# Top-32 attention and two MoE layers on one core: the masking Prelu takes the 32nd score with scale -1, and v's scale is taken off when the transposed x leaves PSUM

## The chip, the cores and the metric

One core of a Trainium2 chip. The metric is the device time of one execution in microseconds (us). Engines: PE = TensorE (matrix multiply), PEld = its weight loads, DVE = VectorE, ACT = ScalarE, POOL = GpSimd, SP = SyncE, which issues the DMAs.

## The reference, cut to what matters

Attention with the 32 largest scores of each row, four batches, eight heads, 576 positions of 64 numbers, then two MoE-like layers on 2304 tokens of 512 numbers:

```
scores = q @ k.T / sqrt(64)
kth    = the 32nd largest score of each row
scores = where(scores >= kth, scores, -1e9)
attn   = exp(scores - max);  attn = attn / (sum(attn) + 1e-9)
x      = attn @ v                              # heads side by side: 2304 x 512
h      = max(x @ w_in, 0);   x = (h * h) @ w_out            # 512 -> 2048 -> 512
out    = max(x @ w1, x @ w2, x @ w3) @ w_out2               # 512 -> 768 -> 512
```

The arithmetic is carried in pairs: a rounded number and what the rounding lost (`xh` and `xl`, `hh` and `hl`, two halves of `wt`, of `qt`, of `e16`, of `vt`), so that three matmuls stand for one.

## The kernel before, in words

**Jobs.** `attend` is called for a unit (some query tiles of one batch) and a pair of heads. A job in it is one tile of 128 queries for one head, or, at the 64 queries that are left over, 64 of each of two heads. There are 144 jobs, 24 for each of six groups. A job runs so:

- TensorE makes 576 scores for each of 128 queries in two halves (L499); ScalarE copies them to `s`, scaled (L426).
- VectorE finds the 32 largest in four rounds: MAX8 writes eight into `mx` (L432), MATCH_REPLACE8 strikes them out in the copy `w` (L434). The 32nd is `mx[:, 31:32]`.
- POOL makes two columns of `nb`: the negated 32nd score (L436), and the 32nd score minus the largest plus a constant (L438).
- ScalarE: Prelu with the bias `nb[:, 0:1]` and the slope 2^110 (L440, recorded as L308): scores at or above the 32nd keep their distance to it, the others become hugely negative. Then Exp with the bias `nb[:, 1:2]` (L442), then a cast to 16 bits (L445).
- POOL makes the lost part of that cast (L446 to L449, recorded as L305, the line of a helper).
- SyncE issues a transposing DMA, `e16` to `et` (L450); TensorE multiplies `et` with `vt` (L461), ScalarE copies the result to `xs` (L464). The first column of `vt` is ones, so `xs` also holds the sums.

**Scale of v.** `prep_v`, once for each of 16 pairs of heads, measures the size of v: ScalarE sums its absolute values (L371), TensorE sums over the partitions (L374), ScalarE copies that to `sc` (L375), and VectorE turns it by bit operations into a power of two that scales v up (L376). ScalarE multiplies v by it (L378) before v is cut into two 16-bit halves. `sc` lives on until the last use of the pair: `finish_x` multiplies the sums by it (L504, on VectorE, with `sc` as a pointer operand, one number for each partition) and takes the reciprocal (L506), and POOL multiplies `xs` by that (L512), so that x is back at its own size in `xg`.

**x.** TensorE transposes `xg` into PSUM (L484; L470 for the left-over queries), ScalarE copies it to `xh` (L486, L473), and VectorE subtracts that copy from PSUM into `xl` (L487 and L474, recorded as L305 with `xt<-b`).

**MoE.** `moe(g)` runs when the x of a group is complete: 654 matmuls (L595) over 28 pieces of weights. For the first group the weights come as 64-bit numbers and are converted on the way, 56 half pieces: ScalarE (L553, recorded as L308 with `cv`), VectorE (L555 and L557), ScalarE (L559), POOL (`wt<-cv,wt`), and the result is also written to DRAM; the other five groups read that.

**What sets the order.** Every operation is handed to `Plan` with its engine, a modelled duration, a priority and the buffers that it reads and writes. `Plan.run` places the operations one after the other where they can start earliest in this model (a hop of some 200 to 280 ns between engines, a small weight for the priority), and the program is then emitted in that order, which `fix_order` keeps on each engine. A buffer kind has a number of slots (`nbufs`: `mx` 4, `nb` 4, `e` 3, `e16` 2, `et` 2, `sc` 6); an operation that opens a buffer waits for the last use of the one that had the slot. So each engine's queue is a fixed list, and the list depends on all modelled durations and on all reads and writes.

Of the kernel before, what the change touches and what calls it, by code (L numbers as in the profile page):

```python
# [10 lines left out]
F32 = mybir.dt.float32  # L11
# [20 lines left out]
LW, LI = 20.0, 0.001  # L32
DROP = 2.0 ** 110
SL = 1000.0
# [228 lines left out]
def kernel(ctx, tc, q, k, v, w_in, w_out, w1, w2, w3, w_out2, out):  # L263
# [8 lines left out]

    nbufs = {"ks": 1, "qs": 1, "vst": 2, "kt": 4, "qt": 1, "vt": 4, "vs": 1, "sm": 2, "sc": 6, "s": 6, "w": 2, "e": 3, "e16": 2,
             "et": 2, "mx": 4, "nb": 4, "rc": 4, "xs": 2, "xr": 2, "xg": 3, "xt": 3, "cv": 3,
# [94 lines left out]
    def prep_v(vst):  # L369
# [4 lines left out]
        pe(A_V, 107.0, [sm], [ps, sc], lambda: nc.tensor.matmul(ps[:, 0:1], ones_t[:], sm[:], start=True, stop=True))  # L374
        act(A_V, 1, [ps], [sc], lambda: nc.scalar.activation(sc[:], ps[:, 0:1], AF.Copy, bias=2.0 ** -100))  # L375
        dve(A_S, 1, [sc], [sc], lambda: nc.vector.tensor_scalar(  # L376
            sc[:].bitcast(U32), sc[:].bitcast(U32), 0x7F800000, 0x7F800000, op0=ALU.bitwise_and, op1=ALU.bitwise_xor))
# [6 lines left out]
            nc.gpsimd, vt[:, :, :, VW2:VW], vs[:], vt[:, :, :, 1:VW2]))  # L384
        return vt, sc

# [14 lines left out]
    def attend(i, unit, p):  # L401
# [7 lines left out]
        if new:  # L409
            kv[b, p] = [kt, *prep_v(load_v(b, p))]  # L410
        kt, vt, sc = kv[b, p]
        if g not in xt:
# [7 lines left out]
        for j, h in jobs:  # L420
            s = buf("s", [P, S])
            for f in range(2):
# [4 lines left out]
                    s[:, cs], ps[:, 0:HS], AF.Copy, scale=escale))  # L427
            w_, mx, nb, e = buf("w", [P, S]), buf("mx", [P, 32]), buf("nb", [P, 2]), buf("e", [P, S])
            for r in range(4):
# [3 lines left out]
                if r < 3:  # L433
                    dve(A_X, S, [src, (mx, r)], [w_], lambda src=src, mx=mx, m8=m8, w_=w_: nc.vector.match_replace(  # L434
                        out=w_[:], in_to_replace=mx[:, m8], in_values=src[:], imm_value=-3.0e38))
            gps(A_E, 1, [(mx, 3)], [(nb, 0)], lambda mx=mx, nb=nb: nc.gpsimd.tensor_scalar(  # L436
                nb[:, 0:1], mx[:, 31:32], -1.0, None, op0=ALU.mult))
            gps(A_E, 1, [(mx, 0), (mx, 3)], [(nb, 1)], lambda mx=mx, nb=nb: nc.gpsimd.tensor_scalar(  # L438
                nb[:, 1:2], mx[:, 31:32], mx[:, 0:1], ebias, op0=ALU.subtract, op1=ALU.add))
            act(A_E, S, [s, (nb, 0)], [e], lambda s=s, e=e, nb=nb: prelu(  # L440
                e[:], s[:], DROP, bias=nb[:, 0:1]), psum=False, ptr=1)
            act(A_E, S, [e, (nb, 1)], [e], lambda nb=nb, e=e: nc.scalar.activation(  # L442
                e[:], e[:], AF.Exp, bias=nb[:, 1:2]), psum=False, ptr=1)
            e16, et = buf("e16", [P, 2 * S], F16), buf("et", [P, 10, P], F16)
# [21 lines left out]
            if j < 0:  # L466
                xr = buf("xr", [P, P])
                finish_x(xs, sc, D, 1, xr, lambda xr=xr: xr[0:D, :].unsqueeze(1))
                ps = buf("b", [P, 512])
                pe(A_X, 107.0, [xr], [ps, (xh, (p, "r")), (xl, (p, "r"))], lambda xr=xr, ps=ps: nc.tensor.transpose(  # L470
                    ps[:, 0:D], xr[0:D, :], ident_t[0:D, 0:D]))
                cs = slice(rcol[b], rcol[b] + D)
                act(A_X, D, [ps], [(xh, (p, "r"))], lambda ps=ps, cs=cs: nc.scalar.copy(xh[:, p, cs], ps[:, 0:D]))  # L473
                dve(A_S, D, [ps, (xh, (p, "r"))], [(xl, (p, "r"))], lambda ps=ps, cs=cs: sub(  # L474
                    nc.vector, xl[:, p, cs], ps[:, 0:D], xh[:, p, cs].bitcast(F32)), slack=SL / 2)
            elif h == 1 and (j % 2 == 1 or j == nt - 1):
                j0 = j - j % 2
                finish_x(xs, sc, P, j + 1 - j0, xg, lambda j0=j0, j=j: xg[:, j0:j + 1, :])
        w = nt * P
        ps = buf("b", [P, 512])  # L480

        def f():
            for c in range(nt):
                nc.tensor.transpose(ps[:, c * P:(c + 1) * P], xg[:, c, :], ident)  # L484
        pe(A_S, 107.0 * nt, [xg], [ps, (xh, (p, col)), (xl, (p, col))], f)
        act(A_S, w, [ps], [(xh, (p, col))], lambda: nc.scalar.copy(xh[:, p, col:col + w], ps[:, 0:w]))  # L486
        dve(A_S, w, [ps, (xh, (p, col))], [(xl, (p, col))], lambda: sub(  # L487
            nc.vector, xl[:, p, col:col + w], ps[:, 0:w], xh[:, p, col:col + w].bitcast(F32)), slack=SL / 2)

# [11 lines left out]

    def finish_x(xs, sc, pn, nt, dst, xo):
        rc = buf("rc", [P, 2, 2, 1])
        dve(A_S, 4, [xs, sc], [rc], lambda: nc.vector.tensor_scalar(  # L504
            rc[0:pn, 0:nt], xs[0:pn, 0:nt, :, 0:1], eguard, sc[0:pn, :], op0=ALU.add, op1=ALU.mult), slack=SL)
        dve(A_S, 4, [rc], [rc], lambda: nc.vector.reciprocal(rc[0:pn, 0:nt], rc[0:pn, 0:nt]))  # L506

        def part(x):
            return xs[0:pn, 0:nt, :, 1 + x * D:1 + (x + 1) * D]
        n = nt * 2 * D  # L510
        gps(A_X, n, [xs], [xs], lambda: nc.gpsimd.tensor_tensor(part(0), part(0), part(1), op=ALU.add))
        gps(A_X, n, [xs, rc], [dst], lambda: nc.gpsimd.tensor_tensor(  # L512
            xo().rearrange("p t (h d) -> p t h d", h=2), part(0),
            rc[0:pn, 0:nt].to_broadcast([pn, nt, 2, D]), op=ALU.mult))
# [237 lines left out]
```

## Time and profile before

| | |
|---|---|
| times of three runs | 1120.74, 1124.24, 1127.41 us; median 1124.24 |
| profiled execution | 1117.19 us, its span 1115.0 us |
| TensorE busy | 962.4 us (86%), weight loads 893.1 (80%) |
| VectorE busy | 887.4 us (80%) |
| ScalarE busy | 743.0 us (67%) |
| GpSimd busy | 676.8 us (61%) |
| mean granted TensorE clock | 0.914 |
| HBM | 200.80 MB read, 34.08 MB written |

The span goes from the first to the last instruction of the program; the execution's own time is a little longer. A share of the span is an average over stages that have different limits, so the shares alone don't name the limit: the page's second part, with 40 slices, shows VectorE full from the start to some 860 us and TensorE full from some 420 us to the end.

### The profile page before, as it was taken

The numbers are of one execution on the slowest core, as the hardware profiler recorded it, in microseconds if no ns is written. First come the engines' busy times: TensorE is split into PE (matmuls) and PEld (weight loads), VectorE is DVE, ScalarE is ACT, GpSimd is POOL, SyncE is SP. The second block draws the span as 40 slices with busy tenths as digits, with TensorE's granted clock in tenths as the row PEclk, the third lists the DMA queues.
The fourth block names the chain that finished last, engine by engine and source line by source line (L and its number), as shares of the span: only waits on it lengthen the run. The fifth ranks groups of instructions, "written<-read, shape, count | busy, mean of one in ns | idle before, by whom it ended". The sixth has DMA issues, their size and how long they took to land.

```text
span 1115.0 us, 18581 instructions
## 1 busy us (share of the span) xinstructions
PE 962.4 (86%) x6116; PEld 893.1 (80%) x6116; DVE 887.4 (80%) x1840; ACT 743.0 (67%) x1572; POOL 676.8 (61%) x979
## 2 busy tenths in 40 slices
PE   3455537977787799999999999999999999999998
PEld 2344426866677589999899999899999999989997
DVE  7999999999999999999999999999999800100020
ACT  7866757778886778887788877887856743123321
POOL 6854668979889768766576777676655531112211
PEclk8555557998888899999999999999999999999999
DMA  7633586789999899999999999989999987776663
GB/s 292 148 79 70 135 278 156 278 244 316 268 283 301 266 360 269 283 293 288 280 270 268 284 288 232 293 230 267 252 264 260 268 256 264 260 257 241 269 245 141
DMA packets 221343, 278.56 MB, mean 250 GB/s; under 512 B 175680, under 2 KB 179776, under 8 KB 199744
## 3 DMA queue, kind: packets, MB, share of 16 engines
q1 hardware_dynamic: 221248, 277.39, 84.5%
q8 instruction: 48, 0.79, 0.3%
q14 instruction: 47, 0.39, 0.1%
HBM read 200.80 MB, written 34.08 MB: 211 GB/s over the span
## 4 chain that ended last, share of the span: by engine, by line
PE 56%; DVE 27%; POOL 5%; issue 4%; ACT 4%; DMA 4%; SPq 0%; POOLq 0%; ACTq 0%; DVEq 0%
PE a L595 35%; PE b L595 13%; DVE mx L432 11%; DVE w L434 9%; PE b L499 4%; PE b L461 4%; DVE cv L557 3%; DMA et<-e 2%; DVE rc L504 1%; POOL wt L305 1%; DVE cv L555 1%; POOL hl L305 1%; POOL e L305 1%; DMA out_dram<-ot 1%; DVE m L646 0%
## 5 line engine op out<-in xcount | busy, mean ns | idle before, releaser
L432 DVE MAX8 mx<-w 128x8 f32<-128x576 f32 x432 | 310.6, 743 | 0.1
L305 POOL TENSOR_TENSOR e<-e,e 128x512 f16<-128x512 f32 (+1 forms) x288 | 213.6, 757 | 72.6 <-ACT e L445 52.4
L595 PE MATMUL a<-xt,wt 128*128 128x384 f32 x1296 | 249.4, 346 | 0.5 <-DVE xt L305 0.3
L595 PE MATMUL b<-xt,wt 128*128 128x384 f32 x1152 | 234.1, 345 | 2.9 <-DVE xt L305 1.2
L595 PEld LDWEIGHTS a<-xt,wt 128*128 128x128 f32 x1296 | 229.8, 193 | 1.4 <-POOL wt L305 0.7
L595 PE MATMUL a<-hh,wt 128*128 128x384 f32 x768 | 225.2, 344 | 0.5 <-ACT hh L621 0.4
L434 DVE MATCH_REPLACE8 w<-mx,w 128x576 f32<-128x576 f32 x288 | 211.9, 738 | 0.0
L595 PEld LDWEIGHTS b<-xt,wt 128*128 128x128 f32 x1152 | 203.8, 192 | 5.2 <-DVE xt L305 1.6
L305 POOL TENSOR_TENSOR hl<-r,hh 128x384 fp32r<-128x384 f32 x96 | 98.4, 1025 | 136.9 <-ACT hh L621 115.6
L499 PE MATMUL b<-kt,qt 128*128 128x288 f32 x640 | 138.3, 345 | 41.5 <-ACT xs L464 12.7
L499 PEld LDWEIGHTS b<-kt,qt 128*128 128x128 f32 x640 | 116.2, 224 | 52.1 <-ACT xs L464 16.5
L461 PEld LDWEIGHTS <-et 128*128 128x128 f16 (+1 forms) x1440 | 85.5, 109 | 79.1 <-DMA et<-e 49.4
L308 ACT ACTIVATE e<-s,nb 128x576 f32<-128x576 f32 x144 | 111.6, 777 | 54.8 <-POOL nb L436 43.6
L461 PE MATMUL b<-vt,et 128*128 128x129 f16 (+3 forms) x1440 | 102.2, 224 | 52.7 <-DMA et<-e 38.3
L595 PEld LDWEIGHTS a<-hh,wt 128*128 128x128 f32 x768 | 142.3, 189 | 1.8 <-ACT hh L621 1.4
L595 PE MATMUL a<-hl,wt 128*128 128x384 f32 x384 | 132.0, 344 | 8.8 <-POOL hl L305 8.6
L426 ACT ACTIVATE s<-b 128x288 f32<-128x288 f32 x288 | 107.2, 408 | 13.2 <-PE b L499 12.2
L442 ACT ACTIVATE e<-e,nb 128x576 f32<-128x576 f32 x144 | 112.1, 778 | 2.4
L434 DVE MATCH_REPLACE8 w<-mx,s 128x576 f32<-128x576 f32 x144 | 106.0, 738 | 0.0
L619 ACT ACTIVATE r<-b 128x384 f32<-128x384 f32 x96 | 47.0, 490 | 88.5 <-PE b L595 86.5
L432 DVE MAX8 mx<-s 128x8 f32<-128x576 f32 x144 | 105.0, 741 | 1.1 <-POOL nb L438 1.1
L445 ACT CAST e<-e 128x576 f16<-128x576 f32 x144 | 97.0, 676 | 9.3 <-DMA et<-e 9.0
(59 smaller groups left out, 1291.1 us busy)
## 6 DMA issues: line engine op xcount, KB each, us to landing
wt<-wsc SPq DMA_DIRECT2D x140, 1024.0 KB, 5.5
wsc<-wt SPq DMA_DIRECT2D x28, 1024.0 KB, 6.1
xt<-in_moe_w_out_dram SPq DMA_DIRECT2D x22, 512.0 KB, 4.9
ks<-in_k_dram SPq DMA_DIRECT2D x16, 576.0 KB, 4.9
xt<-in_moe_w_dram SPq DMA_DIRECT2D x18, 512.0 KB, 4.9
xt<-in_moe_w_in_dram SPq DMA_DIRECT2D x16, 512.0 KB, 5.1
qs<-in_q_dram SPq DMA_DIRECT2D x16, 384.0 KB, 4.1
vst<-in_v_dram SPq DMA_DIRECT2D x16, 320.0 KB, 4.7
```

The lines of the kernel that those rows point to most:

```text
L305: eng.tensor_tensor(out_ap, a, b, op=ALU.subtract)
L308: return nc.scalar.activation(out_ap, src, AF.Prelu, alpha=slope, **kw)
L426: act(A_S, HS, [ps], [(s, f)], lambda s=s, cs=cs, ps=ps: nc.scalar.activation(s[:, cs], ps[:, 0:HS], AF.Copy, scale=escale))
L432: dve(A_X, S, [src], [(mx, r)], lambda src=src, mx=mx, m8=m8: nc.vector.max(out=mx[:, m8], in_=src[:]))
L434: dve(A_X, S, [src, (mx, r)], [w_], lambda src=src, mx=mx, m8=m8, w_=w_: nc.vector.match_replace(out=w_[:], in_to_replace=mx[:, m8], in_va ...
L442: act(A_E, S, [e, (nb, 1)], [e], lambda nb=nb, e=e: nc.scalar.activation(e[:], e[:], AF.Exp, bias=nb[:, 1:2]), psum=False, ptr=1)
L445: act(A_E, S, [e], [(e16, 0)], lambda e=e, e16=e16: nc.scalar.copy(e16[:, S:2 * S], e[:]), psum=False)
L461: nc.tensor.matmul(ps[0:m, 0:wv], et[:, mm_, c0:c1], vt[:, hh, vc, 0:wv], start=x == 0, stop=x == 8)
L499: nc.tensor.matmul(ps[:, 0:HS], a, c, start=m == 0, stop=m == len(seq) - 1)
L557: dve(C_D, 512, [raw, cv], [cv], lambda part=part, cv=cv: nc.vector.scalar_tensor_tensor(cv[:], part(0), 29, cv[:], op0=ALU.logical_shift_ ...
L595: nc.tensor.matmul(o, x, y, start=first and i == 0 and m == 0, stop=last and i == n - 1 and m == 2)
L619: act(MA, N, [ps], [r], lambda r=r, ps=ps: nc.scalar.activation(r[:, 0:N], ps[:, 0:N], AF.Relu))
```

## The change: what it does

- The Prelu takes `mx[:, 31:32]` itself as its bias and multiplies the score by -1, so it works on the 32nd score minus the score. Its slope for negative values is now 2^-100 (`KEEP`), and the Exp multiplies by -2^100, which brings the kept scores back and makes the others hugely negative. POOL's negated column (L436) goes; `nb` has one column. The Prelu reads `mx`, which POOL alone read before.
- `prep_v` makes a second power of two, `us`, from the same sum, by one more operation on VectorE. `sc` is read no more after `prep_v`; it gets 2 slots in place of 6, and `us` gets 6.
- `finish_x` multiplies the sums by the constant 2 in place of `sc`. x thus stays scaled in `xg` and in PSUM.
- When it leaves PSUM, ScalarE's copy to `xh` becomes an activation with the scale `us` (a pointer), and VectorE's subtraction becomes a multiplication by `us` with a subtraction (scalar_tensor_tensor).

```diff
--- before.py
+++ after.py
@@ -30,7 +30,7 @@
 HOP = 180.0
 TICK = 10240.0 / 3.0
 LW, LI = 20.0, 0.001
-DROP = 2.0 ** 110
+KEEP = 2.0 ** -100
 SL = 1000.0
 DBW, DL0, DL1, DTR = 360.0, 1280.0, 900.0, 1500.0
 HP = 1.4
@@ -270,7 +270,7 @@
     ebias = ESHIFT * float(np.log(2.0))
     eguard = 1e-9 * 2.0 ** ESHIFT
 
-    nbufs = {"ks": 1, "qs": 1, "vst": 2, "kt": 4, "qt": 1, "vt": 4, "vs": 1, "sm": 2, "sc": 6, "s": 6, "w": 2, "e": 3, "e16": 2,
+    nbufs = {"ks": 1, "qs": 1, "vst": 2, "kt": 4, "qt": 1, "vt": 4, "vs": 1, "sm": 2, "sc": 2, "us": 6, "s": 6, "w": 2, "e": 3, "e16": 2,
              "et": 2, "mx": 4, "nb": 4, "rc": 4, "xs": 2, "xr": 2, "xg": 3, "xt": 3, "cv": 3,
              "hh": 6, "hl": 6, "r": 2, "m0": 1, "m1": 1, "ot": 2, "wt": 4,
              "b": 4, "a": 4}
@@ -373,6 +373,9 @@
         ps = buf("b", [P, 512])
         pe(A_V, 107.0, [sm], [ps, sc], lambda: nc.tensor.matmul(ps[:, 0:1], ones_t[:], sm[:], start=True, stop=True))
         act(A_V, 1, [ps], [sc], lambda: nc.scalar.activation(sc[:], ps[:, 0:1], AF.Copy, bias=2.0 ** -100))
+        us = buf("us", [P, 1])
+        dve(A_S, 1, [sc], [us], lambda: nc.vector.tensor_scalar(
+            us[:].bitcast(U32), sc[:].bitcast(U32), 0x7F800000, None, op0=ALU.bitwise_and))
         dve(A_S, 1, [sc], [sc], lambda: nc.vector.tensor_scalar(
             sc[:].bitcast(U32), sc[:].bitcast(U32), 0x7F800000, 0x7F800000, op0=ALU.bitwise_and, op1=ALU.bitwise_xor))
         act(A_V, 10 * D, [vst, sc], [vs], lambda: nc.scalar.activation(
@@ -382,7 +385,7 @@
         act(A_V, 10 * D, [vs], [(vt, 1)], lambda: nc.scalar.copy(vt[:, :, :, 1:VW2], vs[:]), psum=False)
         gps(A_V, 10 * D, [vs, (vt, 1)], [(vt, 2)], lambda: sub(
             nc.gpsimd, vt[:, :, :, VW2:VW], vs[:], vt[:, :, :, 1:VW2]))
-        return vt, sc
+        return vt, us
 
     def prep_q(i, unit, p):
         b, tl, rem = unit[:3]
@@ -408,7 +411,7 @@
         plan.bias = 0
         if new:
             kv[b, p] = [kt, *prep_v(load_v(b, p))]
-        kt, vt, sc = kv[b, p]
+        kt, vt, us = kv[b, p]
         if g not in xt:
             t = buf("xt", [P, 2, KD, NW], F32R)
             xt[g] = Half(t, 0), Half(t, 1)
@@ -425,7 +428,7 @@
                 pe(A_S, c_mm(HS) * (2 if j >= 0 else 4), [kt, qt], [ps, (s, f)], scores(j, h, nt, qt, kt, ps, cs))
                 act(A_S, HS, [ps], [(s, f)], lambda s=s, cs=cs, ps=ps: nc.scalar.activation(
                     s[:, cs], ps[:, 0:HS], AF.Copy, scale=escale))
-            w_, mx, nb, e = buf("w", [P, S]), buf("mx", [P, 32]), buf("nb", [P, 2]), buf("e", [P, S])
+            w_, mx, nb, e = buf("w", [P, S]), buf("mx", [P, 32]), buf("nb", [P, 1]), buf("e", [P, S])
             for r in range(4):
                 src = s if r == 0 else w_
                 m8 = slice(8 * r, 8 * r + 8)
@@ -433,14 +436,12 @@
                 if r < 3:
                     dve(A_X, S, [src, (mx, r)], [w_], lambda src=src, mx=mx, m8=m8, w_=w_: nc.vector.match_replace(
                         out=w_[:], in_to_replace=mx[:, m8], in_values=src[:], imm_value=-3.0e38))
-            gps(A_E, 1, [(mx, 3)], [(nb, 0)], lambda mx=mx, nb=nb: nc.gpsimd.tensor_scalar(
-                nb[:, 0:1], mx[:, 31:32], -1.0, None, op0=ALU.mult))
-            gps(A_E, 1, [(mx, 0), (mx, 3)], [(nb, 1)], lambda mx=mx, nb=nb: nc.gpsimd.tensor_scalar(
-                nb[:, 1:2], mx[:, 31:32], mx[:, 0:1], ebias, op0=ALU.subtract, op1=ALU.add))
-            act(A_E, S, [s, (nb, 0)], [e], lambda s=s, e=e, nb=nb: prelu(
-                e[:], s[:], DROP, bias=nb[:, 0:1]), psum=False, ptr=1)
-            act(A_E, S, [e, (nb, 1)], [e], lambda nb=nb, e=e: nc.scalar.activation(
-                e[:], e[:], AF.Exp, bias=nb[:, 1:2]), psum=False, ptr=1)
+            gps(A_E, 1, [(mx, 0), (mx, 3)], [nb], lambda mx=mx, nb=nb: nc.gpsimd.tensor_scalar(
+                nb[:], mx[:, 31:32], mx[:, 0:1], ebias, op0=ALU.subtract, op1=ALU.add))
+            act(A_E, S, [s, (mx, 3)], [e], lambda s=s, e=e, mx=mx: prelu(
+                e[:], s[:], KEEP, bias=mx[:, 31:32], scale=-1.0), psum=False, ptr=1)
+            act(A_E, S, [e, nb], [e], lambda nb=nb, e=e: nc.scalar.activation(
+                e[:], e[:], AF.Exp, bias=nb[:], scale=-1.0 / KEEP), psum=False, ptr=1)
             e16, et = buf("e16", [P, 2 * S], F16), buf("et", [P, 10, P], F16)
             act(A_E, S, [e], [(e16, 0)], lambda e=e, e16=e16: nc.scalar.copy(e16[:, S:2 * S], e[:]), psum=False)
             gps(A_E, 512, [e, (e16, 0)], [(e16, 2)], lambda e=e, e16=e16: sub(
@@ -465,17 +466,18 @@
                     xs[0:m, max(j, 0) % 2, hh, :], ps[0:m, 0:VW]))
             if j < 0:
                 xr = buf("xr", [P, P])
-                finish_x(xs, sc, D, 1, xr, lambda xr=xr: xr[0:D, :].unsqueeze(1))
+                finish_x(xs, D, 1, xr, lambda xr=xr: xr[0:D, :].unsqueeze(1))
                 ps = buf("b", [P, 512])
                 pe(A_X, 107.0, [xr], [ps, (xh, (p, "r")), (xl, (p, "r"))], lambda xr=xr, ps=ps: nc.tensor.transpose(
                     ps[:, 0:D], xr[0:D, :], ident_t[0:D, 0:D]))
                 cs = slice(rcol[b], rcol[b] + D)
-                act(A_X, D, [ps], [(xh, (p, "r"))], lambda ps=ps, cs=cs: nc.scalar.copy(xh[:, p, cs], ps[:, 0:D]))
-                dve(A_S, D, [ps, (xh, (p, "r"))], [(xl, (p, "r"))], lambda ps=ps, cs=cs: sub(
-                    nc.vector, xl[:, p, cs], ps[:, 0:D], xh[:, p, cs].bitcast(F32)), slack=SL / 2)
+                act(A_X, D, [ps, us], [(xh, (p, "r"))], lambda ps=ps, cs=cs: nc.scalar.activation(
+                    xh[:, p, cs], ps[:, 0:D], AF.Copy, scale=us[:]), ptr=1)
+                dve(A_S, D, [ps, us, (xh, (p, "r"))], [(xl, (p, "r"))], lambda ps=ps, cs=cs: nc.vector.scalar_tensor_tensor(
+                    xl[:, p, cs], ps[:, 0:D], us[:], xh[:, p, cs].bitcast(F32), op0=ALU.mult, op1=ALU.subtract), slack=SL / 2)
             elif h == 1 and (j % 2 == 1 or j == nt - 1):
                 j0 = j - j % 2
-                finish_x(xs, sc, P, j + 1 - j0, xg, lambda j0=j0, j=j: xg[:, j0:j + 1, :])
+                finish_x(xs, P, j + 1 - j0, xg, lambda j0=j0, j=j: xg[:, j0:j + 1, :])
         w = nt * P
         ps = buf("b", [P, 512])
 
@@ -483,9 +485,11 @@
             for c in range(nt):
                 nc.tensor.transpose(ps[:, c * P:(c + 1) * P], xg[:, c, :], ident)
         pe(A_S, 107.0 * nt, [xg], [ps, (xh, (p, col)), (xl, (p, col))], f)
-        act(A_S, w, [ps], [(xh, (p, col))], lambda: nc.scalar.copy(xh[:, p, col:col + w], ps[:, 0:w]))
-        dve(A_S, w, [ps, (xh, (p, col))], [(xl, (p, col))], lambda: sub(
-            nc.vector, xl[:, p, col:col + w], ps[:, 0:w], xh[:, p, col:col + w].bitcast(F32)), slack=SL / 2)
+        act(A_S, w, [ps, us], [(xh, (p, col))], lambda: nc.scalar.activation(
+            xh[:, p, col:col + w], ps[:, 0:w], AF.Copy, scale=us[:]), ptr=1)
+        dve(A_S, w, [ps, us, (xh, (p, col))], [(xl, (p, col))], lambda: nc.vector.scalar_tensor_tensor(
+            xl[:, p, col:col + w], ps[:, 0:w], us[:], xh[:, p, col:col + w].bitcast(F32),
+            op0=ALU.mult, op1=ALU.subtract), slack=SL / 2)
 
     def scores(j, h, nt, qt, kt, ps, cs):
         def run():
@@ -499,10 +503,10 @@
                 nc.tensor.matmul(ps[:, 0:HS], a, c, start=m == 0, stop=m == len(seq) - 1)
         return run
 
-    def finish_x(xs, sc, pn, nt, dst, xo):
+    def finish_x(xs, pn, nt, dst, xo):
         rc = buf("rc", [P, 2, 2, 1])
-        dve(A_S, 4, [xs, sc], [rc], lambda: nc.vector.tensor_scalar(
-            rc[0:pn, 0:nt], xs[0:pn, 0:nt, :, 0:1], eguard, sc[0:pn, :], op0=ALU.add, op1=ALU.mult), slack=SL)
+        dve(A_S, 4, [xs], [rc], lambda: nc.vector.tensor_scalar(
+            rc[0:pn, 0:nt], xs[0:pn, 0:nt, :, 0:1], eguard, 2.0, op0=ALU.add, op1=ALU.mult), slack=SL)
         dve(A_S, 4, [rc], [rc], lambda: nc.vector.reciprocal(rc[0:pn, 0:nt], rc[0:pn, 0:nt]))
 
         def part(x):
```

## Rows read from the trace of the kernel before

**Rows 1.** Busy us (instructions) by stretch: PE, PEld, DVE, ACT, POOL; clock, DMA share, GB/s

```profile
0.00:180.00 180.00, 82.87 (x438) 66.89 (x438) 172.31 (x354) 123.02 (x248) 113.88 (x171) 0.60 0.60 165
...
180.00:410.00 230.00, 187.07 (x1135) 167.39 (x1133) 225.37 (x434) 175.53 (x377) 192.58 (x228) 0.90 0.92 278
...
410.00:890.00 480.00, 472.89 (x3307) 445.97 (x3307) 469.79 (x1017) 379.07 (x819) 324.39 (x531) 1.00 0.98 272
...
890.00:1115.00 225.00, 219.54 (x1244) 212.82 (x1242) 19.97 (x37) 65.35 (x131) 45.94 (x50) 1.00 0.68 241
```

**Rows 2.** The chain that ended last, shares by line: 180 to 410, then 410 to 890

```profile
by line: DVE mx L432 13.6%; issue 12.9%; PE a L595 11.6%; DVE w L434 11.0%; DVE cv L557 9.9%; POOL wt L305 6.1%; DVE cv L555 4.2%; DVE rc L504 3.4%; POOL hl L305 3.3%; POOL e L305 3.1%; DMA wsc<-wt 2.0%; PE b L461 1.6%; PE b L499 1.6%; DVE 
...
by line: PE a L595 44.2%; PE b L595 18.8%; PE b L499 7.9%; PE b L461 7.3%; DMA et<-e 5.0%; DVE mx L432 3.0%; DVE w L434 2.3%; DMA out_dram<-ot 1.5%; PE b L484 1.0%; DVE rc L504 0.9%; ACT e L442 0.8%; ACT s L426 0.7%; ACT e L308 0.6%; POOL k
```

**Rows 3.** Busy us by stretch, around the point where TensorE fills

```profile
425.00:450.00 25.00, 25.00 (x176) 24.47 (x175) 24.00 (x53) 22.22 (x49) 18.82 (x26) 1.00 0.93 269
```

**Rows 4.** Lines on DVE before 410 us: count | busy us, mean ns | idle before, releasers

```profile
L557 DVE SCALAR_TENSOR_TENSOR cv<-xt,cv 128x512 uint32<-128x512 uint32 x56 | 58.3, 1045 | 0.1
...
L432 DVE MAX8 mx<-s 128x8 f32<-128x576 f32 x58 | 41.9, 741 | 1.1 <-POOL nb L438 1.1
...
L555 DVE TENSOR_SCALAR cv<-cv 128x512 uint32<-128x512 uint32 x56 | 41.0, 736 | 8.1 <-ACT cv L308 8.1
...
L504 DVE TENSOR_SCALAR rc<-xs,sc 128x2 f32<-128x2 f32 (+2 forms) x25 | 13.3, 532 | 0.4 <-ACT xs L464 0.4
...
L305 DVE TENSOR_TENSOR xt<-b,xt 128x64 fp32r<-128x64 f32 (+2 forms) x20 | 5.9, 299 | 0.2 <-ACT xt L473 0.2
...
L376 DVE TENSOR_SCALAR sc<-sc 128x1 uint32<-128x1 uint32 x9 | 1.3, 140 | 0.0
```

**Rows 5.** Single lines of the kernel: duration ns min/median/max, first and last start us

```profile
L504 DVE TENSOR_SCALAR rc<-xs,sc x64: 199/353/2625, 49.4 to 905.2; 128x2 f32<-128x2 f32 x32, 128x4 f32<-128x4 f32 x16, 64x2 f32<-64x2 f32 x16
...
L555 DVE TENSOR_SCALAR cv<-cv x56: 395/439/2899, 7.4 to 387.7; 128x512 uint32<-128x512 uint32 x56
...
L557 DVE SCALAR_TENSOR_TENSOR cv<-xt,cv x56: 660/854/3126, 8.7 to 388.8; 128x512 uint32<-128x512 uint32 x56
```

**Rows 6.** Timeline around a long L504: start us, duration us, engine, line

```profile
228.97 2.62 DVE L504 TENSOR_SCALAR rc<-xs,sc 64x2 f32<-64x2 f32 x1
...
230.29 1.28 POOL L305 TENSOR_TENSOR wt<-cv,wt 128x512 fp32r<-128x512 f32 x1
```

**Rows 7.** Lines on POOL before 410 us

```profile
L436 POOL TENSOR_SCALAR nb<-mx 128x1 f32<-128x1 f32 x56 | 15.4, 274 | 26.3 <-DVE mx L432 24.1 <-DVE rc L506 1.1
```

**Rows 8.** Timeline: POOL's negation and the Prelu behind it

```profile
23.68 0.22 POOL L436 TENSOR_SCALAR nb<-mx 128x1 f32<-128x1 f32 x1
...
23.93 0.77 ACT L308 ACTIVATE e<-s,nb 128x576 f32<-128x576 f32 x1 [0.55 <-POOL nb L436]
```

**Rows 9.** The page's costliest groups: ScalarE with and without a pointer operand

```profile
L442 ACT ACTIVATE e<-e,nb 128x576 f32<-128x576 f32 x144 | 112.1, 778 | 2.4
...
L445 ACT CAST e<-e 128x576 f16<-128x576 f32 x144 | 97.0, 676 | 9.3 <-DMA et<-e 9.0
```

**Rows 10.** Lines on DVE before 220.2 us: jobs begun

```profile
L432 DVE MAX8 mx<-s 128x8 f32<-128x576 f32 x35 | 25.1, 739 | 0.0
```

**Rows 11.** Timeline of DVE, 218 to 243 us

```profile
220.35 1.45 DVE L432 MAX8 mx<-s 128x8 f32<-128x576 f32 x2 [1.08 <-POOL nb L438]
```

**Rows 12.** Lines on ACT before 219.9 us: Prelus done

```profile
L308 ACT ACTIVATE e<-s,nb 128x576 f32<-128x576 f32 x31 | 23.8, 774 | 25.2 <-POOL nb L436 25.0
```

**Rows 13.** Timeline of ACT, 218 to 246 us: the next two Prelus

```profile
219.96 0.78 ACT L308 ACTIVATE e<-s,nb 128x576 f32<-128x576 f32 x1 [0.86 <-POOL nb L436]
...
227.50 0.78 ACT L308 ACTIVATE e<-s,nb 128x576 f32<-128x576 f32 x1
```

**Rows 14.** Timeline of DVE: first MAX8 of two successive pairs of jobs

```profile
400.68 1.41 DVE L432 MAX8 mx<-s 128x8 f32<-128x576 f32 x2
...
410.32 1.40 DVE L432 MAX8 mx<-s 128x8 f32<-128x576 f32 x2
```

## The prediction, made before the change was run

> **What bounds the kernel now.** I read the busy times by stretch first [rows 1], then the chain that ended last in the middle and late stretches [rows 2]. Three regimes follow one another.
>
> From 0 to 180 us VectorE is busy 172.31 us and TensorE 82.87; from 180 to 410 us VectorE is busy 225.37 of 230 and TensorE 187.07. From 410 to 890 us TensorE is busy 472.89 of 480 at a granted clock of 1.00, and it stays so to the end (219.54 of 225), while VectorE has 19.97 us of work left after 890 us [rows 1]. The reader is to see where the limit changes hands: VectorE first, TensorE last. The chain says the same: of 180 to 410 us it is mixed, with MAX8, replacement and weight conversion on VectorE, conversions on POOL and MoE matmuls; of 410 to 890 us it is MoE matmuls (44.2% and 18.8%) with VectorE's `mx` at 3.0% [rows 2]. By 425 to 450 us TensorE no longer pauses: 25.00 of 25 [rows 3].
>
> So the end is the moment at which TensorE has a full queue (about 410 us) plus 705 us of TensorE work that this change does not touch. That moment is set by VectorE's work up to the last weight conversion (56 of them, all before 410 us [rows 4]). A nanosecond on VectorE before 410 us moves the end; one after it meets a VectorE that is ahead of TensorE and costs nothing until that lead is gone: its last group's x is wanted only when TensorE has finished the group before it. All sums below are therefore VectorE's time before 410 us.
>
> **The change part by part.**
>
> *The scale's partner `us`.* One more one-column operation on VectorE at each preparation of v. The one beside it, L376, takes 140 ns and stands 9 times before 410 us [rows 4]: 9 x 0.140 = +1.3 us. Its ends are 0 and that; an added operation can't give time back.
>
> *The second half of x, now multiply and subtract.* 20 of these run before 410 us and take 5.9 us together [rows 4]. The trace of before has no multiply-subtract with one operand in PSUM. Lower end: nothing more, and nothing less, since each element gets a multiplication besides. Upper end: the rate halves and the pointer is paid besides, 5.9 + 1.2 = +7.1 us. I take the pointer alone: the shortest L504, with a pointer, is 199 ns [rows 5] and L376, with constants, 140 ns [rows 4]: 59 ns, times 20 = +1.2 us. I stay at that end because the bitwise operation of the same kind, L557, does 512 elements in 660 ns at its shortest [rows 5], 1.29 ns for each with everything in it, so the kind itself is not slow.
>
> *The denominators, L504, which lose their pointer.* 25 before 410 us at 532 ns each [rows 4], though the shortest is 199 and the longest 2,625 [rows 5]. If the pointer were what makes them long, they would fall to L376's 140: 25 x 0.392 = -9.8 us. But one of 2.62 us, from 228.97 to 231.59 us, ends with POOL: a subtraction on POOL ran from 230.29 for 1.28 us, to 231.57 [rows 6]. And L555, which has only constants, also goes from 395 to 2,899 ns [rows 5]. So the length is time spent held off by POOL, and constants don't end that. I take the 59 ns: 25 x 0.059 = -1.5 us, the ends being 0 and -9.8.
>
> The Trainium skill has a rule on this, in Advanced Engine Details and Errata, section VectorE Performance Modes (Mode Summary): VectorE's second SBUF port is shared with GpSimd, and an operation in a two-port mode and one on GpSimd block each other. The rows just named agree with it. It speaks against the change's gain: by this rule L504 stays long with constants (-1.5 us), without it -9.8 us would be due.
>
> *POOL loses 144 one-column operations.* Before 410 us they are 56, 15.4 us [rows 7]. POOL is busy 113.88 + 192.58 = 306.5 us there [rows 1], so 5.0% of its work goes. VectorE loses to POOL what its operations take above their shortest: L555 56 x (0.736 - 0.395) = 19.1, L557 56 x (1.045 - 0.660) = 21.6, L504 25 x (0.532 - 0.199) = 8.3 us [rows 4, 5], 49.0 us in all. 5.0% of that is -2.5 us, which I take. Ends: 0, if small operations never hold anything, and -15.4, if each of their microseconds is one in which VectorE stood.
>
> *Prelu without POOL in front.* POOL's negation starts at 23.68 and the Prelu at 23.93 us [rows 8], so each Prelu can start some 0.25 us earlier. That shortens the path from VectorE to the transposing DMA, not VectorE's own queue, which before 410 us waits on POOL's `nb` only once, for 1.1 us [rows 4]. I cost it at 0; what hides it is the full VectorE queue before 410 us and the full TensorE queue after. Were it paid at all, it would be once, at the job that opens the first MoE group. The operation that subtracts the largest score stays on POOL and still gates the Exp.
>
> *ScalarE's two copies out of PSUM get a pointer.* An Exp with a pointer takes 778 ns and a cast of the same width without one 676 [rows 9]: about 0.1 us on 48 instructions, of which only the last pair's copy stands in front of an MoE group. After 410 us TensorE's queue hides it; before, it is 0.1 us, left out. Ends 0 and 0.1.
>
> *mx is held longer.* Until now a job's `mx` (four slots) came free when POOL's second operation had read it; now the Prelu reads it. So the first MAX8 of job n+4 gets a wait for the Prelu of job n. Behind that MAX8 in VectorE's queue stand the other MAX8 steps and the conversions, and for those wait ScalarE, POOL and in the end TensorE. At 220.35 us the 36th and 37th jobs begin, after 35 others [rows 10, 11]. They would wait for the Prelus of the 32nd and 33rd job, 31 Prelus being done before 219.9 us [rows 12]: the one that starts at 219.96 and ends at 220.74 (0.39 us late), and the one that starts at 227.50 and ends at 228.28, where the second MAX8 begins at about 221.0, 7.3 us earlier [rows 11, 13]. Both ends: 0.4 and 7.3 us. I take 0.4, because the list that orders the instructions knows the new reader and has conversions to put there.
>
> Sum: 1.3 + 1.2 - 1.5 - 2.5 + 0.4 = -1.1 us. The profiled execution took 1117.19 us (span 1115.0 and 2.2 around it), so it would take 1116.1. The median of the three runs is 1124.24, 7 us above that execution; the same difference there gives 1123.1. I predict 1123 us.
>
> **The rivals.**
>
> *A. The order of the instructions comes out otherwise.* The order on all engines is written by a list scheduler from modelled times. Each job loses a POOL operation and a hop in front of its Prelu in these, so ties fall differently. VectorE works jobs off in pairs: one pair begins at 400.68 and the next at 410.32 us [rows 14], 9.6 us. What counts is whether a pair is placed before or after the last conversion. For it: 58 jobs begin before 410 us [rows 4], whereas the second MoE group needs only the 48 of its own and the first group, so pairs are free to move. Against it: VectorE's own modelled durations hardly change. A pair later: -1.1 - 9.6 = -10.7, 1113.5 us. A pair earlier: +8.5, 1132.7 us.
>
> *B. The hold on mx decides.* Place: VectorE's queue at 220 to 228 us, in the stretch that sets the end. Price: 7.3 us in place of 0.4, so -1.5 + 7.3 = +5.8, 1130.0 us, slower than before. It decides where the order still puts that MAX8 before its slot's Prelu has ended and nothing in front of it. For it: this MAX8 was already waiting for an `mx` reader, 1.08 us [rows 11], the slots were short there. Against: everything in the list can move.
>
> *C. L504 does shorten with the pointer.* That is -9.8 in place of -1.5: -9.4, 1114.8 us. Against it stands L555.
>
> *That the change does not do what it says*, I give nothing of its own: if the Prelu waits on as it did, my sum stands, since I credit nothing for it.
>
> **How the numbers follow.** A measurement of this kernel tells about 0.5%, 5.6 us, from no change. My forecast, 1123 (own range 1118 to 1128, from the ends of POOL's relief and of the multiply-subtract), has 0.40. A pair later has 0.25: with less to place on POOL, which is busy 192.58 of 230 us in the conversions' stretch [rows 1], conversions more likely move forward than back. A pair earlier has 0.11, B 0.17, C 0.07. Faster: 0.25 + 0.07 = 0.32. Same: 0.40. Slower: 0.17 + 0.11 = 0.28. The range reaches from below A's faster arm to its slower one, 1111 to 1133.
>
> **What would show it.** Right: L504 keeps a mean above 400 ns with the same maximum above 2 us; the multiply-subtract stays within 0.1 us of the subtraction; the new 128x1 operation is near 140 ns; L555 and L557 lose a few per cent; TensorE stops pausing at 400 to 420 us. Wrong: a VectorE wait of several microseconds of `mx` on the Prelu before 410 us (B); the last conversion 5 us or more away from where it was, with another count of jobs before it (A); L504 at a uniform 150 to 200 ns (C); any change of TensorE's pace after 425 us, of which I expect none.

## The result, and the profile after

The changed kernel takes 1109.76 us (median of four runs, 1109.12 to 1110.85), the kernel before 1122.49 beside it (four runs, 1116.97 to 1127.41): a ratio of 0.9889, interval 0.984 to 0.9938. That is 12.7 us faster, where I had said 1123 and a range from 1111.

The profiled execution took 1109.87 us, its span 1108.1. The span of the profile before was 1115.0, so between the two traces only 6.9 us can be looked for: the kernel before scatters over more than 10 us from run to run and its trace is of one of the shorter executions; the changed one scatters over 1.7.

Busy us by stretch in the changed kernel, in the order of [rows 1] (PE, PEld, DVE, ACT, POOL; clock, DMA share, GB/s):

```profile
0.00:180.00 180.00, 83.76 (x449) 67.20 (x450) 172.19 (x360) 124.25 (x252) 109.48 (x145) 0.59 0.62 165
...
180.00:410.00 230.00, 190.83 (x1153) 170.77 (x1152) 226.70 (x444) 181.20 (x385) 187.84 (x203) 0.90 0.93 285
...
410.00:890.00 480.00, 475.65 (x3315) 449.01 (x3314) 463.87 (x1009) 378.46 (x810) 304.07 (x438) 1.00 0.99 273
...
890.00:1115.00 225.00, 212.37 (x1205) 205.51 (x1203) 24.08 (x46) 63.43 (x128) 45.44 (x50) 1.00 0.67 233
```

TensorE did more in each stretch up to 890 us than in [rows 1]: 83.76 for 82.87 us, then 190.83 for 187.07, then 475.65 for 472.89, and so had 212.37 us left after 890 us where it had had 219.54. By 410 us it was 4.7 us further on, and by 890 us 7.4. Of the shorter end, none was made after 890 us. Note the third stretch: TensorE was "full" in both, and yet it did 2.8 us more.

The lines on VectorE before 410 us, which answer [rows 4] (count | busy us, mean ns | idle before):

```profile
L561 DVE SCALAR_TENSOR_TENSOR cv<-xt,cv 128x512 uint32<-128x512 uint32 x56 | 57.1, 1022 | 0.1
...
L435 DVE MAX8 mx<-s 128x8 f32<-128x576 f32 x60 | 43.8, 742 | 0.0
...
L559 DVE TENSOR_SCALAR cv<-cv 128x512 uint32<-128x512 uint32 x56 | 37.2, 668 | 8.5 <-ACT cv L308 7.7 <-POOL nb L439 0.8
...
L508 DVE TENSOR_SCALAR rc<-xs 128x2 f32<-128x2 f32 (+2 forms) x25 | 15.0, 599 | 0.9 <-ACT xs L465 0.9
...
L490 DVE SCALAR_TENSOR_TENSOR xt<-b,us,xt 128x128 fp32r<-128x128 f32 (+1 forms) x12 | 5.1, 424 | 0.7 <-ACT xt L488 0.7
...
L476 DVE SCALAR_TENSOR_TENSOR xt<-b,us,xt 128x64 fp32r<-128x64 f32 x8 | 2.1, 267 | 0.0
...
L377 DVE TENSOR_SCALAR us<-sc 128x1 uint32<-128x1 uint32 x9 | 1.3, 139 | 0.0
```

Each term of the sum has its row here. `us` costs 139 ns nine times, 1.3 us. The multiply-subtracts take 5.1 + 2.1 = 7.2 us for 20, against 5.9. The denominators (L508) are not shorter but longer, 599 ns for 532. The conversions lose 1.2 us (L561) and 3.8 us (L559). No MAX8 waits for `mx` (0.0).

Single lines, duration in ns as minimum, median and maximum, to [rows 5]:

```profile
L508 DVE TENSOR_SCALAR rc<-xs x64: 140/330/2443, 49.8 to 913.5; 128x2 f32<-128x2 f32 x32, 128x4 f32<-128x4 f32 x16, 64x2 f32<-64x2 f32 x16
...
L559 DVE TENSOR_SCALAR cv<-cv x56: 399/461/1485, 7.4 to 385.0; 128x512 uint32<-128x512 uint32 x56
...
L561 DVE SCALAR_TENSOR_TENSOR cv<-xt,cv x56: 659/751/2447, 8.8 to 386.0; 128x512 uint32<-128x512 uint32 x56
```

The shortest denominator fell from 199 to 140 ns, which is the pointer; the longest is still 2,443 ns, with constants alone. That one ends with a subtraction on POOL, at 342.50 and 342.48 us; the 8 of the 64 denominators that no operation on POOL overlaps took 140 to 170 ns:

```profile
339.81 2.67 POOL L305 TENSOR_TENSOR kt<-ks,kt 64x1152 fp32r<-64x1152 f32 x1
...
340.06 2.44 DVE L508 TENSOR_SCALAR rc<-xs 128x2 f32<-128x2 f32 x1
```

Where on the path did the 6.9 us arise? The start of the last MoE matmul of each group (the 654th, counted in the timeline; us from the trace's first instruction):

| group | 0 | 1 | 2 | 3 | 4 | 5 |
|---|---|---|---|---|---|---|
| before | 399.7 | 551.5 | 711.6 | 868.1 | 992.1 | 1110.7 |
| after | 395.0 | 545.0 | 701.5 | 859.1 | 984.6 | 1103.8 |
| difference | -4.7 | -6.5 | -10.1 | -9.0 | -7.5 | -6.9 |

Some 5 us come before 400 us, where VectorE sets the pace; another 5 us between 400 and 710 us, where I had taken TensorE's work as untouched; 3 us are given back after that. Of the 5 us between the ends of groups 0 and 2, 2.2 are shorter pauses of TensorE; for the rest it is busy 3.2 us less there, because 29 fewer of its instructions for the attention fall between these two ends (2095 in all for 2124).

### The profile page after: what moved, and what is told of

The parts are those of the page before. It is cut to its first block, busy times and chain, and to the rows that moved or that the text cites. A ratio compares the mean times of both kernels' runs of the same rounds, so it can differ in the third digit from the quotient of the medians.

```text
span 1108.1 us, 18444 instructions
## 1 busy us (share of the span) xinstructions
PE 962.6 (87%) x6116; PEld 892.5 (81%) x6116; DVE 886.8 (80%) x1856; ACT 747.3 (67%) x1572; POOL 646.8 (58%) x835
## 4 chain that ended last, share of the span: by engine, by line
PE 49%; DVE 34%; DMA 6%; issue 4%; ACT 3%; POOL 3%; SPq 0%; POOLq 0%; ACTq 0%; DVEq 0%
PE a L599 32%; DVE mx L435 14%; DVE w L437 12%; PE b L599 10%; DMA et<-e 5%; PE b L503 3%; PE b L462 3%; DVE cv L561 3%; DVE cv L559 2%; DVE rc L508 1%; DMA xt<-in_moe_w_in_dram 1%; POOL hl L305 1%; POOL e L305 1%; PE b L486 0%; DVE m L650 0%
## 5 line engine op out<-in xcount | busy, mean ns | idle before, releaser
L599 PE MATMUL b<-xt,wt 128*128 128x384 f32 x1152 | 231.5, 344 | 0.4 <-DVE xt L490 0.4
L308 ACT ACTIVATE e<-s,mx 128x576 f32<-128x576 f32 x144 | 111.8, 778 | 58.4 <-DVE mx L435 49.9
L446 ACT CAST e<-e 128x576 f16<-128x576 f32 x144 | 97.2, 676 | 10.1 <-DMA et<-e 9.7
```

Of the source, the lines that this page charges most:

```text
L308: return nc.scalar.activation(out_ap, src, AF.Prelu, alpha=slope, **kw)
L446: act(A_E, S, [e], [(e16, 0)], lambda e=e, e16=e16: nc.scalar.copy(e16[:, S:2 * S], e[:]), psum=False)
L599: nc.tensor.matmul(o, x, y, start=first and i == 0 and m == 0, stop=last and i == n - 1 and m == 2)
```

## The experiments

The prediction's open question was whether the sum of the terms or a newly written order decides. So the first four kernels part the two.

**New instructions, old order** (e1). The list is made from the old entries; only what they emit is changed (new Prelu, Exp and v's scale, not shown here), and `mx` has 16 tiles in place of 4, so that no MAX8 waits for a Prelu:

```diff
-            gps(A_E, 1, [(mx, 3)], [(nb, 0)], lambda mx=mx, nb=nb: nc.gpsimd.tensor_scalar(...))
+            gps(A_E, 1, [(mx, 3)], [(nb, 0)], lambda: None)
...
+        if self.tag == "mx":
+            Buf.made += 1
+            t = f"mx{Buf.made % 16}"
```

> The new instructions in the old order on every engine: the list is made from the old reads, writes and durations, with an empty entry in place of POOL's negation, and mx has 16 tiles behind its 4 modelled slots so that no MAX8 waits for a Prelu. Theory ORDER (the list came out better, the instructions themselves are worth nothing): 1122 us, within 4 of the kernel before. Theory WORK (POOL's 144 missing operations and the earlier Prelu gain the time): 1110 us, within 3 of the changed kernel; L555 and L557 some 5% shorter than before.

Measured: 1117.1 us, 0.9956 (0.994 to 0.9972). Between the two theories: the instructions in the old order, together with the 16 tiles, are worth some 5 us of the 12, not all and not nothing (e9 below takes the tiles' share out). VectorE's lines before 410 us in this run:

```profile
L568 DVE SCALAR_TENSOR_TENSOR cv<-xt,cv 128x512 uint32<-128x512 uint32 x56 | 52.0, 933 | 0.1
...
L566 DVE TENSOR_SCALAR cv<-cv 128x512 uint32<-128x512 uint32 x56 | 43.1, 773 | 10.7 <-ACT cv L312 10.7
...
L515 DVE TENSOR_SCALAR rc<-xs 128x2 f32<-128x2 f32 (+2 forms) x25 | 12.8, 512 | 1.2 <-ACT xs L472 1.2
```

L568, L566 and L515 are the L557, L555 and L504 of [rows 4]: 52.0 + 43.1 + 12.8 = 107.9 us where there were 112.6. That is 4.7 us less, of which the pointer is 1.5. This trace is of one of the shortest of nine executions (1114.78 us), so its sum is not that of the median.

**New order, old negation** (e2). POOL's negation goes back in front of the Prelu, without an entry in the list:

```diff
-            act(A_E, S, [s, (mx, 3)], [e], lambda s=s, e=e, mx=mx: prelu(
-                e[:], s[:], KEEP, bias=mx[:, 31:32], scale=-1.0), psum=False, ptr=1)
+            def negate_prelu(s=s, e=e, mx=mx, ng=ng):
+                nc.gpsimd.tensor_scalar(ng[:], mx[:, 31:32], -1.0, None, op0=ALU.mult)
+                prelu(e[:], s[:], DROP, bias=ng[:])
+            act(A_E, S, [s, (mx, 3)], [e, ng], negate_prelu, psum=False, ptr=1)
```

> The changed kernel's order, with POOL's negation put back in front of each Prelu (as an instruction that the list does not know), the old Prelu with slope 2^110 and the old Exp scale. The second part, v's scale, stays changed. ORDER: 1110 us, at most 2 more than the changed kernel. WORK: 1120 to 1124 us, back to before.

Measured: 1144.94 us, 1.0212 (1.0188 to 1.0237). Both theories missed: this is 35 us slower than the changed kernel and 23 slower than the one before. The trace says why. ScalarE's waits at the Prelu over the whole run (total us, times, longest), in the kernel before, in the changed one and in this one:

```profile
ACT e L308 <- POOL nb L436: 43.6, 28, 4.3
```

```profile
ACT e L308 <- DVE mx L435: 49.9, 38, 3.8
```

```profile
ACT e L308 <- POOL ng L444: 152.9, 120, 3.4
```

The old order knows of the way through POOL and ScalarE waits for it 28 times; in the new order, which puts the Prelu where `mx` is just done, it waits 120 times, for 152.9 us in place of 43.6. Behind each wait stands all that ScalarE has to do. A wait is 1.3 us on average, though the negation takes 0.2: it also stands behind other work in POOL's queue, in a place that the list did not plan. POOL was idle and waiting for `mx` in front of it 40 times in the kernel before and only 14 times here:

```profile
POOL nb L436 <- DVE mx L432: 53.1, 40, 4.9
```

```profile
POOL ng L444 <- DVE mx L435: 15.5, 14, 3.5
```

So this kernel does not show what the order alone would be worth; it shows that the new order loses time when a step that it doesn't know of stands in front of the Prelu.

**Each part alone**, with a list of its own (e3: the Prelu and POOL part; e4: v's scale):

```diff
# e3: prep_v, finish_x and the copies out of PSUM as before
# e4: POOL's negation, the Prelu with DROP and the Exp as before
```

> Only the Prelu's bias and scale and POOL's negation are changed, v's scale is as before; the list is made anew. WORK: 1109 to 1112 us, the whole gain. ORDER: any time from 1108 to 1128, and the order differs from both kernels'.

> Only v's scale is moved, Prelu and POOL's negation are as before; the list is made anew. WORK: 1122 to 1125 us, since this part adds some 2 us to VectorE and nothing else. ORDER: any time from 1108 to 1128.

Measured: e3 1115.2 us, 0.9944 (0.9926 to 0.9962); e4 1119.57 us, 0.9988 (0.9971 to 1.0005). The Prelu part alone is faster, but by half of the whole, where WORK had expected all of it. e4 is no different from the kernel before; its time lies below WORK's range and inside ORDER's. But each has a list of its own, and the next runs show how far a single list scatters, so neither settles the question.

**Is a new list worth anything by itself?** The factor `HP` on the modelled hop is read by the list alone and touches no instruction. Twice six kernels, the one before and the changed one, with it at 1.38 to 1.44:

```diff
-HP = 1.4
+HP = 1.39
```

> The kernel before, its instructions untouched, with the modelled hop between engines 1% shorter (HP 1.39 in place of 1.4), so that the list falls differently. CHANCE (any new list moves the time by as much as the change did, and the new list of the change was a lucky one): from 1108 to 1135, with the four lists of this kind spread over more than 10 us and no gap between the two kernels. SHORTER PATH (the gain comes from the shorter path in front of the Prelu, in the list and on the chip, and a new list alone is worth little): 1119 to 1125.

> The kernel before with the modelled hop 1% longer (HP 1.41). CHANCE: anywhere from 1108 to 1135. SHORTER PATH: 1119 to 1125.

> The changed kernel with the modelled hop 1% shorter. CHANCE: anywhere from 1108 to 1130, on average some 1117, that is 5 us (the work's share as the new instructions in the old order showed it) under the kernel before. SHORTER PATH: 1107 to 1113.

> The changed kernel with the modelled hop 1% longer. CHANCE: anywhere from 1108 to 1130, on average some 1117. SHORTER PATH: 1107 to 1113.

> The kernel before with the modelled hop at 1.38. CHANCE ONLY (the lists of both kernels scatter about means that differ by the work alone, 1.5 to 5 us): 1112 to 1135, the mean of the old lists near 1122. SHORTER PATH (the list gains from the shorter path on average): old lists stay near 1126.

> The kernel before with the modelled hop at 1.42. CHANCE ONLY: 1112 to 1135, mean of the old lists near 1122. SHORTER PATH: old lists near 1126.

> The changed kernel with the modelled hop at 1.38. CHANCE ONLY: 1110 to 1131, the mean of the new lists near 1120. SHORTER PATH: new lists near 1117 or lower, 8 us under the old ones.

> The changed kernel with the modelled hop at 1.42. CHANCE ONLY: 1110 to 1131, mean of the new lists near 1120. SHORTER PATH: new lists near 1117 or lower.

> The kernel before with the modelled hop at 1.44, the sixth old list. CHANCE ONLY: within the old lists' scatter, 1118 to 1131. SHORTER PATH: the same; only the pair decides.

> The changed kernel with the modelled hop at 1.44, the sixth new list. CHANCE ONLY: 1110 to 1128, the means of the two sixes 2 to 5 us apart, the work's share. SHORTER PATH: under 1116, the means 7 us or more apart.

Measured, as median us and as a ratio to the kernel before on the same chip (intervals some 0.002 to 0.003 to either side, 0.005 for the changed kernel's own):

| hop | 1.38 | 1.39 | 1.40 | 1.41 | 1.42 | 1.44 | mean |
|---|---|---|---|---|---|---|---|
| old instructions | 1118.26 | 1130.44 | (before) | 1126.56 | 1126.58 | 1130.52 | |
| ratio | 0.9965 | 1.0072 | 1 | 1.0043 | 1.0041 | 1.0086 | 1.0035 |
| new instructions | 1120.3 | 1127.93 | 1109.76 | 1116.9 | 1117.28 | 1120.0 | |
| ratio | 0.9998 | 1.0045 | 0.9889 | 0.9964 | 0.9961 | 0.9974 | 0.9972 |

With not one instruction changed, a list moves the time by 1.2% among the old (0.9965 to 1.0086, some 14 us) and by 1.6% among the new (some 17 us); the standard deviation of a list is 0.45% and 0.52%. SHORTER PATH as it was first put, by which a new list alone is worth little, is denied: e5 to e8 all lie outside its ranges.

The changed kernel's own list is the best of its six, by 0.7% to the next. The means differ by 0.63%, some 7 us, with a standard error of 0.28%. That the new instructions with their lists are better on average is likely (2.2 standard errors), but six lists don't tell 2 us from 7, and the later expectations of CHANCE ONLY and SHORTER PATH are not parted: the old mean (near 1126 us) and the distance of the means are about where SHORTER PATH had them, e18 is where CHANCE ONLY had it. Taken as they stand, the means split the gain of 1.11% so: 0.63% is the distance of the means, 0.83% is how far the changed kernel's list lies below the mean of its six, and 0.35% goes off because the list of the kernel before was better than its mean too. By this estimate chance has some two fifths.

Where does a list make its time? e5, the same instructions as before, is at 398.3 us with its first MoE group, 1.4 us earlier than the kernel before, and is 14.6 us behind it at the end of the fourth (882.7 for 868.1). TensorE's stretch and its waits from 410 to 890 us, in e5 and then in the kernel before:

```profile
410.00:890.00 480.00, 464.35 (x3236) 437.05 (x3235) 466.28 (x1006) 372.21 (x802) 316.77 (x521) 1.00 0.98 265
...
PE b L461 <- DMA et<-e: 7.8, 7, 1.9
...
PE a L595 <- POOL hl L305: 6.1, 5, 2.9
```

```profile
PE b L461 <- DMA et<-e: 2.9, 3, 1.4
...
PE a L595 <- POOL hl L305: 2.0, 4, 0.7
```

TensorE is busy 464.35 us in place of the 472.89 of [rows 1]: it waits 4.9 us longer for transposed `et` and 4.1 us longer for `hl`, in a stretch that a busy share of 97 or 99% lets one take for full.

**What in the work gains.** Four kernels more. e9 is the control for e1's 16 tiles, with no instruction changed; e10 the Prelu part in the old order; e11 is e1 with the negation left in its place on POOL for nobody; e12 is the changed kernel in its own order with 16 tiles of `mx`:

```diff
# e11 against e1
-            gps(A_E, 1, [(mx, 3)], [(nb, 0)], lambda: None)
+            gps(A_E, 1, [(mx, 3)], [(nb, 0)], lambda mx=mx, nb=nb: nc.gpsimd.tensor_scalar(
+                nb[:, 0:1], mx[:, 31:32], -1.0, None, op0=ALU.mult))
# e9 against before, e12 against after
+            if self.tag == "mx":
+                Buf.made += 1
+                t = f"mx{Buf.made % 16}"
```

> The kernel before, same instructions in the same order, but with 16 tiles for mx behind the 4 slots of the list. This is the control for the first run, which had 16 tiles too. If the tiles gained that run's time: 1116 to 1118 us. If the new instructions did: 1120 to 1122, at most 1 us off the kernel before, since VectorE waited 1.1 us for mx in all.

> The old order with the new Prelu and without POOL's negation, v's scale as before, 16 tiles for mx. If the first part holds all of the work's gain: 1116 to 1118 us, like both parts in the old order. If the second part (denominators without a pointer) shares in it: 1119 to 1121.

> All new instructions in the old order, 16 tiles for mx, and POOL's negation left in its old place though nobody reads it: POOL works as much as before, the Prelu does not wait for it. RELIEF (POOL's missing work gives VectorE its time back): 1120 to 1122 us, like before. PATH (the Prelu's earlier start): 1116 to 1118, like without the negation.

> The changed kernel, same instructions, same order, with 16 tiles for mx, so that no MAX8 waits for a Prelu. If the hold on mx costs the changed kernel time: 1104 to 1108 us (its MAX8 waits 5.5 us in 4 places). If these waits lie where TensorE sets the pace: 1109 to 1111, no change.

Measured:

| kernel | us | ratio to before | interval |
|---|---|---|---|
| e9: old work, 16 tiles | 1118.55 | 0.9973 | 0.9956 to 0.9990 |
| e10: Prelu part, 16 tiles | 1118.95 | 0.9981 | 0.9964 to 0.9998 |
| e11: all, negation idle, 16 tiles | 1120.38 | 0.9989 | 0.9973 to 1.0005 |
| e1: all, 16 tiles | 1117.1 | 0.9956 | 0.9940 to 0.9972 |

The control took half of e1's gain: 16 tiles alone give some 3 us, with an interval from 1.1 to 4.9; VectorE had waited 1.1 us for `mx` [rows 4], which the interval just reaches. MAX8 in e9 over the whole run:

```profile
L436 DVE MAX8 mx<-s 128x8 f32<-128x576 f32 x144 | 105.2, 742 | 0.0
```

That wait is gone (0.0). So of e1's gain the instructions have about 2 us (0.9956 against 0.9973, intervals that overlap). The new order has more: e12 is the changed kernel with the same 16 tiles as e1, and its 0.9902 (0.9884 to 0.992) lies clear of e1's 0.9956 (0.994 to 0.9972), 6 us apart, with the instructions alike and only the order another.

The one pair among the four kernels with the old order that the intervals part, if only just, is e11 and e1: with POOL's unread negations the kernel is 3 to 4 us slower, with the Prelu free of them. That is what RELIEF expected; PATH has nothing that shows. VectorE's lines before 410 us in e11, to be held against those of e1:

```profile
L569 DVE SCALAR_TENSOR_TENSOR cv<-xt,cv 128x512 uint32<-128x512 uint32 x56 | 57.4, 1030 | 0.1
...
L567 DVE TENSOR_SCALAR cv<-cv 128x512 uint32<-128x512 uint32 x56 | 42.1, 757 | 9.0 <-ACT cv L312 9.0
...
L516 DVE TENSOR_SCALAR rc<-xs 128x2 f32<-128x2 f32 (+2 forms) x25 | 11.7, 466 | 1.3 <-ACT xs L473 1.3
```

57.4 + 42.1 + 11.7 = 111.2 us, against 107.9. But e9 and e10 part by the same negation, with v's scale as before and the Prelu freed besides, and there nothing is gained: 1118.55 and 1118.95 us. The three lines in e10, which has no negation:

```profile
L560 DVE SCALAR_TENSOR_TENSOR cv<-xt,cv 128x512 uint32<-128x512 uint32 x56 | 55.1, 989 | 0.1
...
L558 DVE TENSOR_SCALAR cv<-cv 128x512 uint32<-128x512 uint32 x56 | 45.1, 809 | 9.3 <-ACT cv L312 9.3
...
L507 DVE TENSOR_SCALAR rc<-xs,sc 128x2 f32<-128x2 f32 (+2 forms) x25 | 12.9, 514 | 1.3 <-ACT xs L467 1.3
```

They make 113.1 us, and in e9, which has the negation, 111.3. Each trace is one execution (e10's is its longest), and such a sum scatters: e12 has the instructions and the order of the changed kernel and 107.5 us where that has 109.3. So the relief that POOL's missing work gives VectorE shows in one pair and not in the other; the mean of the two is some 1.4 us with a standard error of about 1, by the ratios, so it is not shown. e10 fits neither of its two expectations well: between e9 and e11, it is no different from either.

e12: 1110.78 us, 0.9902 (0.9884 to 0.992), no change to the changed kernel. There a MAX8 does wait for a Prelu, as this row of the changed kernel and two of its timeline show:

```profile
DVE mx L435 <- ACT e L308: 5.5, 4, 1.8
...
448.86 0.76 DVE L435 MAX8 mx<-s 128x8 f32<-128x576 f32 x1 [0.87 <-ACT e L308]
...
476.15 0.76 DVE L435 MAX8 mx<-s 128x8 f32<-128x576 f32 x1 [1.78 <-ACT e L308]
```

```profile
L439 DVE MAX8 mx<-s 128x8 f32<-128x576 f32 x144 | 106.2, 743 | 0.0
```

All four waits (5.5 us) lie between 448 and 477 us, after TensorE has filled; taking them away (0.0 in e12) gave nothing.

## Why the prediction was wrong, point by point

**What failed is a step of the first part: that the end is 410 us "plus 705 us of TensorE work that this change does not touch", so that VectorE's time before 410 us is the whole account.** The list writes the order of all engines over the whole run, and the sum put nothing on a new order. In the changed kernel TensorE was 4.7 us further on by 410 us, where VectorE's own terms together give -0.7 us (1.3 + 1.3 - 3.3), and did 2.8 us more between 410 and 890 us. The last is the sign of being wrong that the prediction had named itself, a change of TensorE's pace after 425 us, "of which I expect none". With the instructions untouched, e5 went from 1.4 us ahead at 400 us to 14.6 behind at 883. A TensorE that is busy 472.89 of 480 us still has its waits for `et` and `hl` in front of it, 2.9 and 2.0 us in the kernel before.

**Rival A, a new order, has the larger part, but by another mechanism than I gave it.** The same instructions take 0.9956 in the old order (e1) and 0.9889 in the new one (0.9902 with e1's tiles): 6 to 8 us of the 12.7 hang on the order. A had about the right size in its faster arm (1113.5 us, given 0.25), but by a pair of jobs that moves past the last conversion, so that was luck. Nothing of the kind happened: 55 jobs begin before the last conversion in the changed kernel and 54 before, the conversion comes 2.8 us earlier, not 9.6. A new list scatters by a standard deviation of half a per cent, 5 to 6 us. Where two lists are compared, each with this scatter, the difference has one of 0.7%, and a change of no work falls within 5.6 us in little more than one case of two. So the 0.40 for no change was too high, and the range was too narrow on the fast side.

**The sum of the work, -1.1 us, is not contradicted.** In the old order the work is about 2 us (e1 against its control e9, 0.9956 and 0.9973), an estimate that could be 0 or 4. By term:

- `us`: 1.3 us forecast, 9 x 139 ns = 1.3 measured.
- Multiply-subtract: +1.2 forecast, 7.2 - 5.9 = +1.3 measured, or 59 ns more on the 64-column ones (267 ns now, 208 before), as much as the pointer costs L504. The rate is not halved. The row before:

```profile
L305 DVE TENSOR_TENSOR xt<-b,xt 128x64 fp32r<-128x64 f32 x8 | 1.7, 208 | 0.2 <-ACT xt L473 0.2
```

- Denominators: the pointer's 59 ns is exact at the minimum (199 to 140). But the mean rose to 599 ns, so the term is +1.7 us in this trace, not -1.5: the time that they are held off by POOL is larger than what they cost, and scatters (11.7 us in e11's trace, 15.0 here, for the same 25 operations). Rival C did not happen, as L555 had said. The rule of the Trainium skill that the prediction cites (Advanced Engine Details and Errata, section VectorE Performance Modes) has the two engines block each other, and the trace agrees: 2,443 ns for two numbers per partition without a pointer, ending with POOL's subtraction.
- POOL's relief: -2.5 forecast. No run shows it clearly: 3 to 4 us between e11 and e1, nothing between e9 and e10. In the changed kernel's own trace the three lines take 57.1 + 37.2 + 15.0 = 109.3 us for 112.6, and 1.5 of these 3.3 us are the pointer's.
- Prelu's earlier start, costed at 0: e11 has it, and gains nothing by it that shows in the old order. In the new order it is a condition, as e2 shows, since the list had counted on it.
- ScalarE's pointer: 0.1 us on each copy forecast; the median copy of 64 columns went from 212 ns in the kernel before to 316 in the changed one, while a cast became an activation (minimum, median and maximum of each, in that order):

```profile
L473 ACT CAST xt<-b x16: 196/212/232, 187.7 to 790.7; 128x64 fp32r<-128x64 f32 x16
```

```profile
L474 ACT ACTIVATE xt<-b,us x16: 298/316/353, 190.7 to 794.6; 128x64 fp32r<-128x64 f32 x16
```

The Trainium skill (ScalarE: Activation LUTs, section What ACT_TABLE_LOAD costs) gives about 93 ns for each pointer operand; the trace has 104.

- The hold on `mx` (rival B): 0.0 us before 410 us, 5.5 us after, where 0.4 was forecast, and e12 shows that those after cost nothing. Before 410 us the list had left no MAX8 in front of its Prelu, as I took it to.

**What stays open.** The traces of the changed kernel and of the one before lie 6.9 us apart, the medians 12.7. The rest is in the slower executions of the kernel before, of which no trace was taken; why some orders scatter over 10 us from run to run and the changed one over 2 was not tried. Nor is it shown whether the new order is better by luck or because the shorter path in front of the Prelu makes lists better: the two means are 0.63 +- 0.28% apart, some 7 us, and the work in the old order is about 2.

## What to carry to other kernels

Where a planner writes the order of all engines, a change of a modelled duration or of a dependence is two changes: measure the order's own scatter first, by moving a number that the chip never sees, and price the edit against that. Freeze the old order (emit the new instructions from the old entries) to see what the work is worth. And hold a gain that one pair of kernels shows against a second pair that differs in the same thing: here the relief from 144 short operations on GpSimd was 3 to 4 us in one and nothing in the other.

## What the runs showed of the hardware that was not expected

An operation on two numbers per partition took up to 2,443 ns on VectorE while POOL ran, and 140 to 170 when it did not. A subtraction on VectorE with one operand in PSUM cost 59 ns more as a multiply-subtract with a pointer, on 64 columns. And one order of the same instructions took up to 1.6% longer than another.
